# mLSTM cell and mixture of depths on one core: state products moved next to the product with P, second gates spread over two steps, operands on ScalarE, a reordered tail

## The chip, the core and the metric

The kernel runs on one core of a Trainium2 chip. The time is that of the device for one launch, in microseconds; seven runs of the kernel before had a median of 219.94 us (218.05 to 221.98). Profiles come from one further execution, taken by the hardware profiler; its times are in us unless ns is written.

The core's engines, as the profile names them: PE (TensorE, matrix products; PEld is its load of the stationary operand), DVE (VectorE), ACT (ScalarE), POOL (GpSimd) and SP (SyncE, which here only issues DMAs). Each engine works through its own instructions in order, so an instruction that waits holds up all that stand behind it on the same engine.

## What is computed

Two stages. The first is an mLSTM cell over B = 4 batches, H = 8 heads, S = 768 tokens and head size D = 40:

```python
for t in range(S):
    m_new = np.maximum(f_gate[:, :, t] + m, i_gate[:, :, t])
    f_stab = np.exp(f_gate[:, :, t] + m - m_new)
    i_stab = np.exp(i_gate[:, :, t] - m_new)
    m = m_new
    C = f_stab[..., None, None] * C + i_stab[..., None, None] * np.einsum('bhd,bhe->bhde', vt, kt)
    n = f_stab[..., None] * n + i_stab[..., None] * kt
    h_tilde = np.einsum('bhde,bhe->bhd', C, qt)
    denom = np.maximum(np.abs(np.einsum('bhd,bhd->bh', n, qt)), 1.0)[..., None]
    y[:, :, t] = sigmoid(o_gate[:, :, t]) * h_tilde / denom
```

The second takes x = y with the heads side by side (B, S, 320). Each token gets a score, `x @ w_gate`; in each batch the 128 tokens of the highest score go through two dense layers (320 to 1024 to 320) and are replaced by `x + sigmoid(score) * (relu(x @ w1) @ w2)`; the others leave as they are.

## The kernel before

**Tiles.** A batch is cut into six chunks of 128 tokens. Chunk c of batch b is step n = 6b + c; there are 24 steps. Inside a chunk the recurrence is written as a product: `pS` = keys times queries (line 313), a weight matrix W per head with exponents from the gates, `P = pS * W` (line 319, VectorE), and `pH = P v` (line 367). What comes from earlier chunks is the state C: `pIC` holds C times the queries (line 339) and the chunk's own contribution to C (line 345). `num` on VectorE adds both (lines 349 and 374), lines 377 to 380 make the reciprocal of the denominator, `sor` on POOL multiplies it with the output gate (line 382), `x` (line 387) is the result, stored from SP, and `scr`/`sc` (line 390) its score.

**The gates.** They are scanned along tokens for 96 rows at once (three chunks of 32 heads), in two groups g = 0 and 1: running sums and maxima (lines 177 to 179), `ends`, `carry` and `carried` through PE, `level`, then `split` into three bfloat16 parts. `operands` (line 222) makes from these parts, by a product into `pO`, two operands per chunk and half of the batches: `a_o` (ScalarE) and `M_o` (VectorE, line 234). `weights` multiplies them (`pW`, line 291) and takes exponentials on ScalarE; `causal` on POOL zeroes what lies ahead in time (line 297). `columns` transposes the scales; `scaled_v` (POOL, line 304) gives `wv` for the state, and `decay` (POOL, line 327) scales C ahead of the addition on VectorE (lines 357 and 359).

**Selection and layers.** `spread` transposes the score column on PE (`pb`, line 396) and ScalarE copies it; `compare` counts in step n + 1 how many tokens lie above (line 403). At c = 0 of the next batch `columns_of`, `ranks` and `select` turn the counts into ranks and a selection matrix; at c = 1 `gather` makes the indices (`pidx`, line 431) and an indirect DMA on POOL fetches the 128 rows `xe`; at c = 2 they are transposed (`pX`, line 451); from c = 3 `first` (line 471, `ph`) and, in the batch after that, `second` (line 480, `py`) run a few products a step in `layer`; `leave` writes the rows back at c = 2. The last batch does all of this behind its last step. `warm` (line 173) are products whose result nobody reads, in steps without layer work.

**Order.** The schedule is written out by hand: each engine's instructions stand in the order in which the code issues them, and the tile pools put in the waits. In step n of the kernel before the order is: P(n), W(n+2) with causal and wv, state products and num of step n, decay, layer, pH(n), pb(n-1), transposes `pt` of step n+2 (line 271), pS(n+1), norm, compare, x, select or gate, operands. On-chip buffers matter: the PSUM pool `ps_m` has two buffers for pO, pb, ph, py, pX, pcol and pidx; `ps_t` two for pt and pW; `ps_h` one for pH and the warm products. Loads are issued four steps ahead, and the weights w1 and w2 in steps 3 to 7.

**Shapes on PE.** pH, pIC and the chunk's part of the state use all 128 rows and 64 columns at a time (128*64 in the profile), pS uses 64 rows (64*128), pW and pO 32 rows (32*128), and the rest the full array (128*128). All but pW, pO, warm, pcol and the steps' pidx are float32.

Of the kernel before, what the change touches and what calls it, by code (L numbers as in the profile page):

```python
# [27 lines left out]
def kernel(  # L28
# [127 lines left out]

    FM = [gate.tile([NR, 2, L], FP, name=f"FM{g}") for g in range(2)]
# [17 lines left out]
    def scans(g):  # L175

        nc.vector.tensor_tensor_scan(out=FM[g][:, 0], data0=ones, data1=f_sb[g], initial=0.0, op0=OP.mult, op1=OP.add)
        nc.vector.tensor_tensor(out=a[g], in0=i_sb[g], in1=FM[g][:, 0], op=OP.subtract)
        nc.vector.tensor_tensor_scan(out=FM[g][:, 1], data0=ones, data1=a[g], initial=-BIG, op0=OP.mult, op1=OP.max)

# [41 lines left out]
    def operands(u, c):  # L222
# [4 lines left out]
        for j in (1, 0):  # L227
            for part in range(3):
# [5 lines left out]
        nc.vector.scalar_tensor_tensor(out=M_o[u, c], in0=pO[0].unsqueeze(1).to_broadcast([128, 4, L]),  # L234
                                       scalar=of[:, 1:2], in1=which.unsqueeze(2).to_broadcast([128, 4, L]),
                                       op0=OP.add, op1=OP.mult)

    def columns(g):
# [3 lines left out]
        for j, row in enumerate((wk[g], r[g], r[g][:, L - 1:L].to_broadcast([NR, L]))):  # L242
            nc.tensor.transpose(pc[:, j, :], row, ident[0:NR, 0:NR])
        both = const.tile([128, 3, NR], FP, name=f"cols{g}")
# [86 lines left out]
    def exchange(b, c, qk, T, wv):  # L331
# [9 lines left out]
        if c < NT - 1:  # L341

            for p in range(NP):
                for j, e in enumerate(HALVES):
                    nc.tensor.matmul(pC[e, p, :], qk[:, 0, 2 * p + j, :], wv[:, 2 * p + j, :], start=True, stop=True)  # L345
        num = None
# [81 lines left out]
    def gather(b, sel, token):  # L428
        pidx = ps_m.tile([K_, 1], FP, name="pidx", tag="m")
        for t in range(NT):  # L430
            nc.tensor.matmul(pidx, sel[:, t, :], token[:, t:t + 1], start=(t == 0), stop=(t == NT - 1))
        idx = mod.tile([K_, 1], U32, name="idx")
# [79 lines left out]
    def layer(b, c):  # L512

        if b > 0 and c == 1:
            picked[b - 1] = gather(b - 1, sel[b - 1], token)
        elif b > 0 and c == 2:
# [14 lines left out]
        elif c == 4:  # L531
            layers[b - 1].first(3, 7)
        else:
            layers[b - 1].first(7, NFC)
            layers[b - 1].second(0, 5)

    def step(n):
        b, c = steps[n]
        qk, v1, so = loaded[n]
        load(n + AHEAD)  # L540
        P = weighted(pS[n], W[n])
        if n + 2 < N:
            W[n + 2] = weights(*steps[n + 2])
            causal(W[n + 2])
            stated(n + 2)
        num = exchange(b, c, qk, T[n], wv[n])
        if n + 1 < N:
            decay(*steps[n + 1])
        layer(b, c)
        pH = within(P, v1)  # L550
        pb, pc = steps[n - 1]
        spread(pc, *state[pb][1][:2])
# [181 lines left out]
```

## Time and profile before

| | |
|---|---|
| median of seven runs | 219.94 us (218.05 to 221.98) |
| the profiled execution | 217.27 us |
| its span, first to last instruction | 214.80 us |
| PE busy | 188.9 us (88%) |
| DVE busy | 139.4 us (65%) |
| POOL busy | 99.3 us (46%) |
| ACT busy | 94.1 us (44%) |
| mean granted clock of PE | 0.956 |
| start of pH in steps 1, 6, 12, 18, 23 | 29.7, 64.9, 110.7, 150.8, 185.9 us |

A line of the timeline gives the start, the length, the engine, the source line, the operation, output <- inputs, the shape and how many instructions are taken together; in brackets stands how long the engine was idle before and which instruction it waited for. Matmuls overlap, so the difference of two starts says more than a length. A row `PEclk` holds the clock that PE was granted, in 40 equal slices of the span (5.37 us each), 9 for full speed.

### The profile page before, as it was taken

What the parts mean: (1) busy time and instruction counts of PE and PEld (TensorE: products, weight loads), DVE (VectorE), ACT (ScalarE), POOL (GpSimd) and SP (SyncE); (2) the same over time, 40 slices, a digit from 0 to 9 for tenths busy, and PEclk for the clock granted to TensorE, in tenths of its full rate; (3) what the DMA queues carried; (4) which work ended last, traced back from release to release, by engine and by line L of the source; (5) the groups of instructions that cost most, each with busy time, mean ns of one, the idle gap of its engine ahead of it and who ended that gap; (6) DMA issues with size and microseconds to landing.
All of it is one profiled execution on the core that took longest, in us unless ns stands there. A gap on an engine that the chain in (4) does not pass through costs nothing.

```text
span 214.8 us, 6507 instructions
## 1 busy us (share of the span) xinstructions
PE 188.9 (88%) x2611; PEld 152.2 (71%) x2611; DVE 139.4 (65%) x414; ACT 94.1 (44%) x212; POOL 99.3 (46%) x152
## 2 busy tenths in 40 slices
PE   7978698797898949999999999999999999848991
PEld 2556476675677737889877879988878899638970
DVE  6655737669877962856778668676786875662101
ACT  5762816443664441654645543566525541100110
POOL 6172547445556571344476555554585441021101
PEclk9987859999999995999999999999999999999998
DMA  4899994796999899759599897589992010000100
GB/s 84 119 169 145 149 170 90 95 132 171 134 197 171 212 169 220 125 56 146 104 160 137 129 124 158 94 137 140 142 136 69 34 61 3 31 32 34 31 0 31
DMA packets 105854, 24.37 MB, mean 113 GB/s; under 512 B 100640, under 2 KB 105248, under 8 KB 105824
## 3 DMA queue, kind: packets, MB, share of 16 engines
q1 hardware_dynamic: 105296, 22.60, 69.2%
q0 software_dynamic: 384, 1.31, 2.0%
q8 instruction: 20, 0.33, 0.8%
q14 instruction: 10, 0.08, 0.1%
q10 hardware_dynamic: 144, 0.05, 0.1%
HBM read 19.37 MB, written 4.59 MB: 112 GB/s over the span
## 4 chain that ended last, share of the span: by engine, by line
PE 63%; DVE 12%; issue 10%; DMA 5%; POOL 5%; ACT 2%; POOLq 1%; DVEq 0%
PE pH L367 12%; PE pS L313 9%; PE ph L471 8%; PE pt L271 7%; PE pIC L339 6%; PE py L480 6%; PE pw L173 5%; DMA xe<-out_dram,idx 4%; POOL sor L382 4%; PE pIC L345 4%; PE pW L291 3%; PE pb L396 2%; DVE x L387 1%; DVE scr L390 1%; DVE sel L425 1%
## 5 line engine op out<-in xcount | busy, mean ns | idle before, releaser
L382 POOL TENSOR_TENSOR sor<-so,rec 128x320 f32<-128x320 f32 x24 | 24.2, 1007 | 49.3 <-DVE rec L380 45.0
L297 POOL TENSOR_SCALAR_AFFINE_SELECT W<-W 128x512 f32<-128x512 f32 x48 | 31.5, 681 | 29.8 <-ACT W L292 29.8
L367 PEld LDWEIGHTS pH<-v,P 128*64 128x64 f32 x768 | 27.0, 148 | 12.2 <-PE pw L173 6.1
L397 ACT COPY sb<-pb 128x128 f32<-128x128 f32 x24 | 6.4, 266 | 64.1 <-PE pb L396 56.6
L367 PE MATMUL pH<-v,P 128*64 128x64 f32 x768 | 30.4, 237 | 3.4 <-PE pw L173 1.6
L319 DVE TENSOR_TENSOR P<-pS,W 128x512 f32<-128x512 f32 x48 | 30.7, 680 | 0.0
L292 ACT ACTIVATE W<-pW 128x512 f32<-128x512 f32 x48 | 26.0, 594 | 6.4 <-PE pW L291 5.1
L272 ACT COPY T<-pt 128x512 f32<-128x512 f32 x48 | 25.9, 588 | 5.8 <-PE pt L271 5.8
L313 PE MATMUL pS<-T 64*128 64x128 f32 x384 | 27.9, 285 | 0.0
L271 PE MATMUL pt<-ident,qk 128*128 128x128 f32 x192 | 26.1, 280 | 0.7 <-ACT W L292 0.7
L313 PEld LDWEIGHTS pS<-T 64*128 64x128 f32 x384 | 23.3, 187 | 4.0 <-issue 3.9
L374 DVE TENSOR_TENSOR num<-num,pH 128x328 f32<-128x328 f32 x20 | 9.9, 496 | 23.0 <-PE pH L367 23.0
L471 PE MATMUL ph<-xeT,w 128*128 128x128 f32 x192 | 24.1, 280 | 0.3 <-DVE idx L433 0.3
L271 PEld LDWEIGHTS pt<-ident,qk 128*128 128x128 f32 x192 | 22.6, 145 | 1.5 <-ACT W L292 1.0
L471 PEld LDWEIGHTS ph<-xeT,w 128*128 128x128 f32 x192 | 22.2, 192 | 1.0 <-issue 0.4
L480 PE MATMUL py<-w,hT 128*128 128x320 f32 x64 | 19.1, 438 | 0.0
L387 DVE TENSOR_TENSOR x<-num,sor 128x320 f32<-128x320 f32 x20 | 9.8, 492 | 13.2 <-POOL sor L382 13.2
L339 PE MATMUL pIC<-C,T 128*64 128x82 f32 x320 | 16.4, 246 | 0.0
L339 PEld LDWEIGHTS pIC<-C,T 128*64 128x64 f32 x320 | 13.0, 140 | 4.2 <-issue 2.5
L403 DVE SCALAR_TENSOR_TENSOR ge<-sb,sc,earlier 128x128 bf16<-128x128 f32 (+5 forms) x24 | 15.4, 643 | 0.8 <-ACT sb L397 0.8
L327 POOL TENSOR_TENSOR C<-C,cols 128x328 f32<-128x328 f32 x16 | 11.8, 736 | 6.8 <-DVE C L359 5.7
L173 PE MATMUL pw<-earlier 128*128 128x512 bf16 x38 | 13.5, 470 | 1.6 <-POOL earlier L98 1.6
(124 smaller groups left out, 265.2 us busy)
## 6 DMA issues: line engine op xcount, KB each, us to landing
qk<-in_k_dram SPq DMA_DIRECT2D x24, 160.0 KB, 3.4
qk<-in_q_dram SPq DMA_DIRECT2D x24, 160.0 KB, 4.0
v<-in_v_dram SPq DMA_DIRECT2D x24, 160.0 KB, 4.4
so<-in_o_gate_dram SPq DMA_DIRECT2D x24, 160.0 KB, 4.4
out_dram<-x SPq DMA_DIRECT2D x24, 160.0 KB, 2.2
w<-in_moe_w_dram SPq DMA_DIRECT2D x2, 640.0 KB, 4.7
w<-in_moe_w_dram SPq DMA_DIRECT2D x2, 512.0 KB, 3.9
w<-in_moe_w_dram SPq DMA_DIRECT2D x1, 256.0 KB
```

What stands on the lines that cost most here:

```text
L173: nc.tensor.matmul(pw, earlier[:, 0:128], earlier[:, 0:4 * L], start=True, stop=True)
L271: nc.tensor.transpose(pt[:, p, :], qk[:, j, 2 * p:2 * p + 2, :].rearrange("s a d -> s (a d)"), ident)
L272: nc.scalar.copy(out=T[:, j], in_=pt)
L292: nc.scalar.activation(out=W[:, h0:h0 + 4, :], in_=pW, func=AF.Exp)
L297: nc.gpsimd.affine_select(out=W[:, h0:h0 + 4, :], in_=W[:, h0:h0 + 4, :], compare_op=OP.is_ge, fill=0.0, base=0, pattern=[[0, 4], [1, L]], ...
L313: nc.tensor.matmul(pS[j][:, p, :], T[e, 0, p, :], T[e, 1, p, :], start=True, stop=True)
L319: nc.vector.tensor_tensor(out=P[:, :, j, :], in0=pS[j], op=OP.mult, in1=W.rearrange("p (n a) t -> p n a t", a=2)[:, :, j, :])
L339: nc.tensor.matmul(pI[t, 2 * p * D1:2 * (p + 1) * D1], T[:, 1, p, t], C[:, p].rearrange("e a d -> e (a d)"), start=True, stop=True)
L367: nc.tensor.matmul(pH[t, 2 * p + j, :], P[:, p, j, t], v1[:, 2 * p + j, :], start=True, stop=True)
L382: nc.gpsimd.tensor_tensor(out=sor, in0=so, in1=rec.unsqueeze(2).to_broadcast([128, H, D]), op=OP.mult)
L471: nc.tensor.matmul(self.ph[:, f % 4, :], w1[:, j, f * 128:(f + 1) * 128], self.xeT[:, j, :], start=(j == 0), stop=(j == NDC - 1))
L480: nc.tensor.matmul(self.py, self.hT[:, f, :], w2[:, f, :], start=(f == 0), stop=(f == NFC - 1))
```

## The change

The order of a step is turned: step n begins with pH(n), directly behind it come the state products of step n+1 (`exchange`, now without its VectorE part, which is `exchanged`), decay(n+1) and pS(n+1). Then W(n+2) and operands, norm, compare, x, then columns_of or gather, layer, pt(n+2), pb(n) (one step earlier than it was), and at the end P(n+1), num(n+1) and the addition to C. In steps 1 to 3 W(n+2) is computed late, behind pb. Nine of the twelve M_o (chunks 3 to 5 of the first two batches, all of the last two) are made by four ScalarE activations, one per head (`beside=False`). The second group's gates, which stood ahead of step 1, are cut into pieces that run inside steps 0 and 1. The placement matrices for the second half of the batches are built behind step 2 instead of step 1. In the tail, `leave` of batch 2 and a second selection matrix in half precision stand ahead of the copies, and the indices come from the latter.

The diff, with one line around each changed place:

```diff
                                 in_=ident.rearrange("p (g x) -> p g x", x=32)[:, :, 12 * j:12 * j + 12])
+    of_which = const.tile([128, 4], FP, name="of_which")
+    nc.vector.tensor_scalar(out=of_which, in0=which, scalar1=of[:, 1:2], scalar2=None, op0=OP.mult)
     FM = [gate.tile([NR, 2, L], FP, name=f"FM{g}") for g in range(2)]
...
             nc.tensor.matmul(pw, earlier[:, 0:128], earlier[:, 0:4 * L], start=True, stop=True)
-    def scans(g):
+    def sums(g):
         nc.vector.tensor_tensor_scan(out=FM[g][:, 0], data0=ones, data1=f_sb[g], initial=0.0, op0=OP.mult, op1=OP.add)
         nc.vector.tensor_tensor(out=a[g], in0=i_sb[g], in1=FM[g][:, 0], op=OP.subtract)
+    def maxima(g):
         nc.vector.tensor_tensor_scan(out=FM[g][:, 1], data0=ones, data1=a[g], initial=-BIG, op0=OP.mult, op1=OP.max)
...
         nc.scalar.activation(out=r[g], in_=FM[g][:, 1], func=AF.Exp, bias=m_in[g], scale=-1.0)
-    def operands(u, c):
+    def operands(u, c, beside=True):
         g, own = c // 3, slice(c % 3 * BH, c % 3 * BH + BH)
...
         nc.scalar.activation(out=a_o[u, c], in_=pO[1], func=AF.Identity, bias=of[:, 0:1], scale=1.0)
-        nc.vector.scalar_tensor_tensor(out=M_o[u, c], in0=pO[0].unsqueeze(1).to_broadcast([128, 4, L]),
-                                       scalar=of[:, 1:2], in1=which.unsqueeze(2).to_broadcast([128, 4, L]),
-                                       op0=OP.add, op1=OP.mult)
+        if beside:
+            nc.vector.scalar_tensor_tensor(out=M_o[u, c], in0=pO[0].unsqueeze(1).to_broadcast([128, 4, L]),
+                                           scalar=of[:, 1:2], in1=which.unsqueeze(2).to_broadcast([128, 4, L]),
+                                           op0=OP.add, op1=OP.mult)
+        else:
+            for h in range(4):
+                nc.scalar.activation(out=M_o[u, c][:, h], in_=pO[0], func=AF.Identity, scale=which[:, h:h + 1],
+                                     bias=of_which[:, h:h + 1])
     def columns(g):
...
             nc.tensor.transpose(pc[:, j, :], row, ident[0:NR, 0:NR])
+        return pc
+    def keep(g, pc):
         both = const.tile([128, 3, NR], FP, name=f"cols{g}")
...
                     nc.tensor.matmul(pC[e, p, :], qk[:, 0, 2 * p + j, :], wv[:, 2 * p + j, :], start=True, stop=True)
+        return pI, pC
+    def exchanged(b, c, pI, pC):
         num = None
...
                                 in1=rank[:, t0:t1].unsqueeze(2).to_broadcast([128, t1 - t0, K_]), op=OP.is_equal)
-    def gather(b, sel, token):
+    def number(sel, token):
         pidx = ps_m.tile([K_, 1], FP, name="pidx", tag="m")
...
             nc.tensor.matmul(pidx, sel[:, t, :], token[:, t:t + 1], start=(t == 0), stop=(t == NT - 1))
+        return pidx
+    def gather(b, pidx):
         idx = mod.tile([K_, 1], U32, name="idx")
...
     def layer(b, c):
-        if b > 0 and c == 1:
-            picked[b - 1] = gather(b - 1, sel[b - 1], token)
-        elif b > 0 and c == 2:
+        if b > 0 and c == 2:
             layers[b - 1] = Layers(b - 1, *picked[b - 1])
...
         elif c == 4:
-            layers[b - 1].first(3, 7)
+            layers[b - 1].first(3, NFC)
         else:
-            layers[b - 1].first(7, NFC)
             layers[b - 1].second(0, 5)
-    def step(n):
+    def weighed(n):
+        causal(W[n])
+        stated(n)
+    def step(n, **more):
         b, c = steps[n]
-        qk, v1, so = loaded[n]
+        _, v1, so = loaded[n]
         load(n + AHEAD)
-        P = weighted(pS[n], W[n])
-        if n + 2 < N:
+        pH = within(P[n], v1)
+        for f in more.get("carry", ()):
+            f()
+        if n + 1 < N:
+            give = exchange(*steps[n + 1], loaded[n + 1][0], T[n + 1], wv[n + 1])
+            decay(*steps[n + 1])
+            pS[n + 1] = products(T[n + 1])
+        late = 0 < n < NT - 2
+        if 1 < n < NT - 2:
+            operands(0, n + 2, beside=False)
+        if n + 2 < N and not late:
             W[n + 2] = weights(*steps[n + 2])
-            causal(W[n + 2])
-            stated(n + 2)
-        num = exchange(b, c, qk, T[n], wv[n])
-        if n + 1 < N:
-            decay(*steps[n + 1])
+        if 4 <= n < 4 + NT:
+            operands(1, n - 4, beside=False)
+        num, sor = norm(nums.get(n), pH, so)
+        for f in more.get("sor", ()):
+            f()
+        if n > 0:
+            pb, pc = steps[n - 1]
+            compare(pc, *state[pb][1])
+        if c == 0:
+            state[b] = open_batch()
+        result(b, c, num, sor, state[b][0])
+        for f in more.get("result", ()):
+            f()
+        if b > 0 and c == 0:
+            pcol = columns_of(state[b - 1][1][2])
+        elif b > 0 and c == 1:
+            picked[b - 1] = gather(b - 1, number(sel[b - 1], token))
         layer(b, c)
-        pH = within(P, v1)
-        pb, pc = steps[n - 1]
-        spread(pc, *state[pb][1][:2])
         if n + 2 < N:
...
             gated(n + 2)
+            if not late:
+                weighed(n + 2)
+        spread(c, *state[b][1][:2])
+        if late:
+            W[n + 2] = weights(*steps[n + 2])
         if n + 1 < N:
-            pS[n + 1] = products(T[n + 1])
-        num, sor = norm(num, pH, so)
-        compare(pc, *state[pb][1])
-        if b > 0 and c == 0:
-            pcol = columns_of(state[b - 1][1][2])
-        if c == 0:
-            state[b] = open_batch()
-        result(b, c, num, sor, state[b][0])
+            P[n + 1] = weighted(pS[n + 1], W[n + 1])
+            nums[n + 1] = exchanged(*steps[n + 1], *give)
+        for f in more.get("end", ()):
+            f()
+        if late:
+            weighed(n + 2)
         if b > 0 and c == 0:
...
                 layers[b - 2].leave()
-        if n + 3 < NT:
-            operands(0, n + 3)
-        if 3 <= n < 3 + NT:
-            operands(1, n - 3)
     state[0] = open_batch()
...
     load(4)
-    pS = {}
+    P, pS, nums, kept = {}, {}, {}, {}
     warm(8)
-    scans(0)
+    sums(0)
+    maxima(0)
     ends(0)
...
     turn(loaded[0][0], 1, T[0])
-    columns(0)
+    operands(0, 1)
     W[0] = weights(0, 0)
-    warm(1)
+    keep(0, columns(0))
+    weighed(0)
     pS[0] = products(T[0])
-    operands(0, 1)
-    causal(W[0])
-    stated(0)
     gated(0)
-    scans(1)
-    P = weighted(pS[0], W[0])
+    P[0] = weighted(pS[0], W[0])
     W[1] = weights(0, 1)
-    split(1, 1, 0, nc.gpsimd.tensor_copy, nc.gpsimd)
-    split(1, 1, 1, nc.gpsimd.tensor_copy, nc.gpsimd)
-    causal(W[1])
-    ends(1)
+    weighed(1)
     turned(1)
-    warm(1)
-    exchange(0, 0, loaded[0][0], T[0], wv[0])
-    carry(1)
-    pH = within(P, loaded[0][1])
+    give = exchange(0, 0, loaded[0][0], T[0], wv[0])
+    exchanged(0, 0, *give)
     operands(0, 2)
-    pm = carried(1)
-    pS[1] = products(T[1])
-    num, sor = norm(None, pH, loaded[0][2])
-    stated(1)
-    decay(0, 1)
-    level(1, pm)
-    W[2] = weights(0, 2)
-    split(1, 0, 0, nc.scalar.copy, nc.vector)
-    result(0, 0, num, sor, state[0][0])
-    split(1, 0, 1, nc.scalar.copy, nc.vector)
-    causal(W[2])
-    stated(2)
-    scales(1)
     gated(1)
-    turned(2)
-    operands(0, 3)
-    columns(1)
-    gated(2)
     nc.gpsimd.affine_select(out=earlier[:, S - L:], in_=earlier[:, S - L:], compare_op=OP.is_gt, fill=0.0, base=0,
                             pattern=[[-1, L]], channel_multiplier=1)
-    for n in range(1, N):
+    def parts_of_a():
+        for half in range(2):
+            split(1, 1, half, nc.gpsimd.tensor_copy, nc.gpsimd)
+    def level_and_split():
+        level(1, kept["pm"])
+        scales(1)
+        split(1, 0, 0, nc.vector.tensor_copy, nc.vector)
+    def rest_of_M():
+        split(1, 0, 1, nc.vector.tensor_copy, nc.vector)
+        operands(0, 3, beside=False)
+        kept["pc"] = columns(1)
+    step(0, sor=[lambda: sums(1), parts_of_a], result=[lambda: maxima(1), lambda: ends(1)], end=[lambda: carry(1)])
+    step(1, carry=[lambda: kept.update(pm=carried(1))], sor=[level_and_split], result=[rest_of_M],
+         end=[lambda: keep(1, kept["pc"])])
+    for n in range(2, N):
         step(n)
-        if n == 1:
+        if n == 2:
             for j in range(2):
...
             nc.vector.tensor_copy(out=token, in_=token_i)
-            token_f = const.tile([128, NT], FP, name="token_f")
-            nc.vector.tensor_copy(out=token_f, in_=token_i)
             later = const.tile([128, NT], FP, name="later")
-            nc.vector.tensor_scalar(out=later, in0=token_f, scalar1=-1.0, scalar2=float(S - 1), op0=OP.mult, op1=OP.add)
+            nc.vector.tensor_scalar(out=later, in0=token_i, scalar1=-1.0, scalar2=float(S - 1), op0=OP.mult, op1=OP.add)
             ones_b = const.tile([128, 1], BF, name="ones_b")
...
     own = layers[b - 1]
-    spread(u, sc, sb)
     compare(u, sc, sb, ge, cnt)
...
             nc.tensor.matmul(pX[0:w, j, :], x_t[b, t][:, d0:d0 + w], sel[:, t], start=(t == 0), stop=(t == NT - 1))
+    own.leave()
+    sel_h = mod.tile([128, NT, K_], HF, name="sel", bufs=1)
+    select(sel_h, rank, 0, NT)
     nc.scalar.copy(out=last.xeT[:, 0:NDC - 1], in_=pX[:, 0:NDC - 1])
     nc.scalar.copy(out=last.xeT[0:w, NDC - 1], in_=pX[0:w, NDC - 1])
-    own.leave()
-    last.idx, last.xe = gather(b, sel, token_f)
+    last.idx, last.xe = gather(b, number(sel_h, token))
     last.first(0, NFC)
```

## The prediction

> Steps are numbered n = 0 to 23 (six per batch); pH(n) is step n's product with P, "state" the two blocks L339/L345 (pIC and pC). Times are us of the span.
>
> **What bounds the kernel now.** I first read the busy times and the clock row of the page: PE is busy 88%, but its clock was halved three times (slices 3 to 6, 16 and 17; the tails of the row are full speed).
>
> ```profile
> PE 188.9 (88%) x2611; PEld 152.2 (71%) x2611; DVE 139.4 (65%) x414; ACT 94.1 (44%) x212; POOL 99.3 (46%) x152
> PEclk9987859999999995999999999999999999999998
> ```
>
> Then the chain in order of time, for the starts of pH: pH(0) 16.2, pH(1) 29.7, then 37.8, 45.2, 52.5, 58.8, 64.9, 72.4, 82.7, 91.8, 98.9, 104.7 and pH(12) 110.7; pH(18) 150.8; pH(23) 185.9; end 214.8. So there are four regimes, each with its own limit. Steps with expert layers are full on PE; the timeline of one:
>
> ```profile
> 98.78 1.15 PE L367 MATMUL pH<-v,P 128*64 128x64 f32 x32
> 99.86 0.32 PE L396 MATMUL pb<-ident,sc 128*128 128x128 f32 x1
> 100.02 1.04 PE L271 MATMUL pt<-ident,qk 128*128 128x128 f32 x8
> 100.99 1.16 PE L313 MATMUL pS<-T 64*128 64x128 f32 x16
> 102.08 0.39 PE L291 MATMUL pW<-M_o,a_o 32*128 32x512 bf16 x2
> 102.40 0.79 PE L339 MATMUL pIC<-C,T 128*64 128x82 f32 x16
> 103.12 1.60 PE L471 MATMUL ph<-xeT,w 128*128 128x128 f32 x12
> 104.65 1.15 PE L367 MATMUL pH<-v,P 128*64 128x64 f32 x32
> ```
>
> Differences of starts are what each block costs: pH 1.08, pb 0.16, pt 0.97, pS 1.09, pW 0.32, pIC 0.72, ph 1.53 (2.21 for x18). No gap is left. The shape changes six times in a step, and the first instructions behind a change are slower: inside the pt block six transposes take 0.65 (100.02 to 100.67), so eight should take 0.87, not 0.97; inside ph two take 0.22, so 18 should take 1.98, not 2.21.
>
> In batch 0 PE waits. There a loop on VectorE closes through PE: scr(n), M_o 0.74, pW, pIC, state, warm, pH(n+1), num:
>
> ```profile
> 42.04 0.75 DVE L234 SCALAR_TENSOR_TENSOR M_o<-pO,of,which 128x512 bf16<-128x512 f32 x1
> 42.84 0.39 PE L291 MATMUL pW<-M_o,a_o 32*128 32x512 bf16 x2 [1.25 <-DVE M_o L234]
> ```
>
> At n=8 PE waits for a gather, and the clock falls behind it (pH(8) takes 2.0 instead of 1.1):
>
> ```profile
> 74.83 1.23 POOL L435 DMA_INDIRECT xe<-out_dram,idx  x1 [0.36 <-DVE den L378]
> 80.49 0.88 PE L451 MATMUL pX<-ident,xe 128*128 128x128 f32 x3 [3.15 <-DMA xe<-out_dram,idx]
> ```
>
> The tail is a chain on PE: pX 4.3, pidx 1.5, ph 5.5, py 4.5, then ye and its write.
>
> ```profile
> 198.26 1.50 PE L431 MATMUL pidx<-token_f,sel 128*128 128x1 f32 x12
> 200.10 5.60 PE L471 MATMUL ph<-xeT,w 128*128 128x128 f32 x48 [0.34 <-DVE idx L433]
> ```
>
> **The change, stage by stage.**
>
> *Shapes.* In the new order pH(n), pIC(n+1) and state(n+1) share one shape, and ph, pt, pb another: pH/pIC/pC, pS, pW, full block. Four changes instead of six. The two that go are pW to pIC and pH to pb. By the excesses above a change costs 0.10 (pt block) to 0.23 (ph block, both ends); I take 0.15 each, 0.3 a step. Two new pairs (state to pS, pW to ph) are in no row; bounds for the sum are 0 and 0.45 (two at the larger excess).
> The Trainium skill (TensorEngine Tiling (Array Packing), Key Properties) says that a change of tiling mode drains the array, which agrees and gives no price; by it alone the sum would stay open.
>
> *Steady steps.* A full step is then pH 1.07 + pIC 0.56 + state 0.45 + pS 1.09 + pW 0.30 + ph 2.19 + pt and pb 0.98 = 6.64 (was 6.99). It holds only if VectorE's loop is shorter: after P(n) ends, L349 and C take 1.06 (0.41 + 0.65), num 0.53, den/den/rec 0.6, sor on POOL 1.0 to 1.4 with its hand-overs 0.15, x and scr 1.05, P(n+1) 1.2: 5.5 to 5.9. Hidden under PE in full steps. By c: c=0: pcol 0.79 and py 1.75 in place of ph: 7.0. There pb now waits for rank, since pcol holds the other of two buffers; rank stands behind P, num and C on VectorE, about 6.65 after P(n), and pH(n+1) is queued behind pb. PE arrives there at 6.9, so py covers it; uncovered it costs up to 1. c=1: 6.67. c=2: 6.26. c=3: ye and scre moved behind P, so the write of ye (1.04 on POOL) and decay 0.74 stand before sor: 7.2, not 6.64. c=4 (no state): 6.19. c=5 (ph x12, no pIC): 5.42 on PE, 5.5 on VectorE. Batch sum 38.8 against 40.1 (110.7 to 150.8). Steps 18 to 22: 7.0+6.67+6.26+7.2+6.4 = 33.5 against 35.1.
>
> *Operands.* Nine of twelve M_o go from VectorE (0.74) to ScalarE: four activations of 128x128, by the a_o row (0.36) 1.44, bounds 1.1 and 1.5. VectorE's loop in batch 0 loses 0.74. But in n=4 to 9 a_o and M_o stand behind two exponentials (1.1), and what comes next on PE (pcol, pidx, pX, ph) needs a_o's buffer: pO done at 3.9 behind the start of pH, a_o at 4.6, hence 0.7 of PE wait in n=6 to 9 (bounds 0 and 0.9). T follows M_o on ScalarE and is now wanted 1.2 after pt: about 0.1 late.
>
> *Start.* Without the second gates PE reaches pH(0) at 14.5, pH(1) at 21 (was 29.7): P(0) no longer stands behind the scans (it began at 13.38; now at 11.6, behind causal). In step 0 the scans (1.1) and in step 1 level and splits (1.9) stand on VectorE's chain; pO(3) waits for M's last split until 26.5, M_o until 28.3, T copies to 29.65, pW(3), pH(2) at 30.1 (was 37.8).
>
> *Steps 2 to 4.* Here the lead goes back. In the late steps pW(n+2) comes behind pt and shares its two buffers: it waits for T's copies (0.7 behind pt). Its exponentials stand on ScalarE behind so (0.95) and sb (0.27); then causal (0.65 behind) and wv (0.74) on POOL. From pt: 0.7+0.95+0.27+1.1+0.65+0.74 = 4.4. State(n+2), in front of pS on PE, wants wv at 2.6: 1.8 of PE wait, where the trace of before has none. A step is then 8.3 to 8.8. Places (33.59 to 35.88 before: 2.3 on POOL) moved one step later, in front of decay and sor(3): that step 9.7. The three casts behind n=3 (0.31+0.62+0.6) wait for iota behind causal: step 4 7.9. pH(3) 38.9, pH(4) 48.6, pH(5) 56.5 (was 58.8).
>
> *Queues and small things.* SP's order stays: load(n+4), x, then w1 or w2; x and the loads behind it move with the steps, qk of n+1 is read a step earlier, and a load has two steps before pt wants it (landing 3.4 to 6.4), so I cost it at nothing, though w2's second half now leaves beside the gather. of_which (one VectorE row of 0.15) falls into the wait for f_sb (0.63); the removed cast token_f (0.16) and two warm products (0.39 each) are inside the sums.
>
> *Steps 5 to 11.* 5: 5.85 (VectorE). 6: 7.3 (pO 0.42 and rank). 7: 6.75. 8: 6.7 and 0.95 of waits. 9: 6.64+0.42+0.7 = 7.76. 10: 6.19. 11: 5.5. The gather now leaves at the end of step 7 (idx behind scr) instead of in its middle; pX comes 5.4 behind it, and the trace's one loaded gather took 5.66, so 0.3 of wait instead of 3.15, bounds 0 and 3. pH(9) 84.1 (was 91.8), pH(12) 103.5 (was 110.7).
>
> *Tail.* With the half-precision sel and token pidx costs what it does in the steps (0.30 for x6 at 71.32) instead of 1.50. The new select (0.96) and ye stand beside pX (4.3). ph then waits for xeT (198.99): 1.1 earlier.
>
> **The sum.**
>
> | | before | after |
> |---|---|---|
> | pH(2) | 37.8 | 30.1 |
> | pH(5) | 58.8 | 56.5 |
> | pH(9) | 91.8 | 84.1 |
> | pH(12) | 110.7 | 103.5 |
> | pH(18) | 150.8 | 142.3 |
> | pH(23) | 185.9 | 175.9 |
> | end | 214.8 | 203.7 |
>
> That is at full clock. Before, the clock was halved in 14.9 to 18.3, 25.1 to 31.9 and 79.7 to 86.5, each time behind about 3.4 us in which PE was busy some 55% or less (the stretch 77.4 to 80.5 shows no matmul at all). After, steps 1 to 4 have such stretches (24.6 to 26.5, 31.7 to 33.5, 40.5 to 42.2). pH(1), 2.0 for 1.1, prices one halving at 1.5 to 3. I take 3 in sum, bounds 0 and 8.
> The Trainium skill (TensorE: Matmul & The Clock Gate, Part 1) says that an idle window of about 3.4 us halves the clock and a busy one of that length gives it back; it speaks against this change, which adds idle time to steps 1 to 4. By its wording a partly busy window might cost nothing or all, so by it the span would lie anywhere from 203.7 to 211.7.
>
> So span 206.7, and with the 2.47 around it (217.27 - 214.80) 209.2, 3.7% under the profiled 217.27. That execution lies under all seven runs (218.05 to 221.98); scaled to their median 219.94 it is 211.7. I say **211.5**.
>
> **Rivals.**
> 1. *Forecast* (0.48): 207 to 215.
> 2. *Clock holds and wv comes in time* (0.16): 203.7 + 2.5, scaled, is 208.7; without the 0.7 waits in n=6 to 9 and half the 1.8 waits 204. For it: more PE work between gaps in the start.
> 3. *The lead of the start is given back whole* (0.14): halved clock in each of steps 1 to 4 (8) and the gather late by 3: 203.7+8+2.7 = 214.4, with the ends 216.9, scaled 219.5. No change.
> 4. *Slower: the clock stays low* (0.22). Place: from step 1 to pH(9), where ph begins. Before, the busy stretch 25.1 to 28.5 with small gaps did not give the clock back; the new waits for wv, T and a_o leave gaps in every such step. If it stays halved past pH(4), each of steps 4 to 8 costs some 3 more: 203.7+3+15 = 221.7, 224.2 with the ends, scaled 227. It decides from the third halved step on. Against it: steps 5 to 8 are nearly full on PE by the sums above, and the before kernel recovered in two stretches.
>
> A change of under 1% is what a measurement of this kernel hardly tells from none. Cases 1 and 2 are faster and 4 is slower; of case 3's 0.14 I put 0.02 to faster, 0.11 to same and 0.01 to slower: faster 0.66, same 0.11, slower 0.23. The range takes in case 2, the forecast and case 3: 204 to 221.
>
> **What would show it.** pIC directly behind pH with no slow first rows; steps of 6.6 at c=3, 4 in batch 1, and 7.2 at c=3 of batch 2; PE waiting in front of L358 for wv in steps 2 and 3 (right: 1 to 2); pb at c=0 waiting for rank by little; pX at n=8 waiting under 1; pidx at 0.3. I am wrong if the clock row shows more than three halved slices, if ScalarE ends waits in the steady steps, or if the gather still ends a wait of 3.

## Result and the profile after

The changed kernel takes **209.75 us** (median of 20 runs, 208.13 to 211.28), the kernel before 219.14 (48 runs, 215.80 to 222.57): a ratio of 0.9617, 95% interval 0.9590 to 0.9644. The ratio, here and in the experiments, compares only runs within 1.5% of the fastest of their kernel; 209.75 over 219.14 would be 0.957. The forecast was 211.5, with a range of 204 to 221. The profiled execution of the changed kernel has a span of 208.2 us at a mean granted clock of 0.969 and took 210.24 us.

First the page: the rows of busy time and of the granted clock (40 slices, tenths of full speed).

```profile
PE 183.6 (88%) x2606; PEld 150.3 (72%) x2606; DVE 143.6 (69%) x408; ACT 102.8 (49%) x246; POOL 100.1 (48%) x152
...
PEclk9999966999999999969999999999999999999997
```

PE is as busy a share of a shorter span. Two places are slower in the clock row, slices 6 and 7 and slice 18; before there were three.

Then the chain of PE, one step with experts (n = 10, the step that was shown of before; start, duration, engine, line):

```profile
94.13 1.15 PE L383 MATMUL pH<-v,P 128*64 128x64 f32 x32
95.11 0.74 PE L352 MATMUL pIC<-C,T 128*64 128x82 f32 x16
95.78 1.16 PE L326 MATMUL pS<-T 64*128 64x128 f32 x16
96.88 0.39 PE L304 MATMUL pW<-M_o,a_o 32*128 32x512 bf16 x2
97.19 2.27 PE L491 MATMUL ph<-xeT,w 128*128 128x128 f32 x18
99.31 1.04 PE L284 MATMUL pt<-ident,qk 128*128 128x128 f32 x8
100.18 0.27 PE L412 MATMUL pb<-ident,sc 128*128 128x128 f32 x1
100.38 1.15 PE L383 MATMUL pH<-v,P 128*64 128x64 f32 x32
```

By differences of starts: pH 0.98 (was 1.08), pt 0.87 (0.97), ph for 18 products 2.12 (2.21). The blocks whose neighbour now has their own shape are each 0.1 shorter.

The waits of PE that answer to those of before, from its timeline (in brackets the idle time ahead, and what ended it):

```profile
42.86 0.67 PE L358 MATMUL pIC<-wv,qk 128*64 128x41 f32 x16 [1.50 <-POOL wv L317]
...
82.14 0.55 PE L471 MATMUL pX<-ident,xe 128*128 128x128 f32 x3 [1.36 <-ACT a_o L238]
...
89.31 3.90 PE L491 MATMUL ph<-xeT,w 128*128 128x128 f32 x18 [1.16 <-ACT a_o L238]
...
192.81 0.30 PE L448 MATMUL pidx<-token,sel 128*128 128x1 f16 x6
193.46 5.59 PE L491 MATMUL ph<-xeT,w 128*128 128x128 f32 x48 [0.34 <-ACT xeT L734]
```

The 3.15 us for the gather are gone from pX; in their place stands 1.36 for a_o. The same kind of wait stands ahead of pcol (1.14), pidx (1.36) and ph (1.16), and behind the last the clock is halved: 3.90 for what takes 2.27 a step later.

Where the 6.6 us of span went, by the starts of pH:

| stretch | before | after | difference | forecast (full clock) |
|---|---|---|---|---|
| to pH(5) | 58.8 | 55.9 | -2.9 | 56.5 |
| pH(5) to pH(9) | 33.0 | 28.3 | -4.7 | 27.6 |
| pH(9) to pH(12) | 18.9 | 21.8 | +2.9 | 19.4 |
| pH(12) to pH(18) | 40.1 | 39.9 | -0.1 | 38.8 |
| pH(18) to pH(23) | 35.1 | 34.4 | -0.7 | 33.6 |
| pH(23) to the end | 28.9 | 27.8 | -1.1 | 27.8 |

The forecast's column sums to 203.7; with its 3 us for the clock it was 206.7, against 208.2.

### The profile page after: what moved, and what is told of

It is laid out like the page before. It is cut to its first block, busy times and chain, and to the rows that moved or that the text cites. A ratio compares the mean times of both kernels' runs of the same rounds, so it can differ in the third digit from the quotient of the medians.

```text
span 208.2 us, 6517 instructions
## 1 busy us (share of the span) xinstructions
PE 183.6 (88%) x2606; PEld 150.3 (72%) x2606; DVE 143.6 (69%) x408; ACT 102.8 (49%) x246; POOL 100.1 (48%) x152
## 4 chain that ended last, share of the span: by engine, by line
PE 34%; DVE 18%; issue 10%; POOL 7%; ACT 3%; DMA 3%; POOLq 1%; ACTq 0%
PE pH L383 7%; PE ph L491 6%; PE pS L326 5%; PE pt L284 4%; POOL sor L398 4%; PE py L500 3%; DVE P L332 3%; PE pIC L352 3%; ACT W L305 3%; DVE scr L406 2%; DVE x L403 2%; DVE num L390 2%; DVE ge L419 2%; DVE den L394 2%; DMA out_dram<-ye,idx 1%
## 5 line engine op out<-in xcount | busy, mean ns | idle before, releaser
L310 POOL TENSOR_SCALAR_AFFINE_SELECT W<-W 128x512 f32<-128x512 f32 x48 | 32.7, 704 | 30.9 <-ACT W L305 30.5
L383 PEld LDWEIGHTS pH<-v,P 128*64 128x64 f32 x768 | 25.7, 141 | 7.6 <-DVE P L332 2.7
L383 PE MATMUL pH<-v,P 128*64 128x64 f32 x768 | 29.2, 230 | 1.9 <-DVE P L332 1.9
L491 PE MATMUL ph<-xeT,w 128*128 128x128 f32 x192 | 25.4, 292 | 1.5 <-ACT a_o L238 1.2
L491 PEld LDWEIGHTS ph<-xeT,w 128*128 128x128 f32 x192 | 23.7, 203 | 3.2 <-issue 1.4
L403 DVE TENSOR_TENSOR x<-num,sor 128x320 f32<-128x320 f32 x20 | 11.1, 553 | 12.7 <-POOL sor L398 12.7
L419 DVE SCALAR_TENSOR_TENSOR ge<-sb,sc,earlier 128x128 bf16<-128x128 f32 (+5 forms) x24 | 17.9, 746 | 1.0 <-ACT sb L413 1.0
L317 POOL TENSOR_TENSOR wv<-v,cols 128x328 f32<-128x328 f32 x20 | 15.0, 751 | 0.0
L358 PE MATMUL pIC<-wv,qk 128*64 128x41 f32 x320 | 12.9, 230 | 1.9 <-POOL wv L317 1.9
L406 DVE CUSTOM_DVE_ANT_0 scr<-x,wg 128x320 f32<-128x320 f32 x24 | 14.0, 582 | 0.8
```

The lines of the kernel that those rows point to most:

```text
L310: nc.gpsimd.affine_select(out=W[:, h0:h0 + 4, :], in_=W[:, h0:h0 + 4, :], compare_op=OP.is_ge, fill=0.0, base=0, pattern=[[0, 4], [1, L]], ...
L383: nc.tensor.matmul(pH[t, 2 * p + j, :], P[:, p, j, t], v1[:, 2 * p + j, :], start=True, stop=True)
L419: nc.vector.scalar_tensor_tensor(out=ge[:, GE[u]:GE[u + 1]], in0=sb.rearrange("p t l -> p (t l)")[:, 0:n], scalar=sc[:, u:u + 1], in1=earl ...
L491: nc.tensor.matmul(self.ph[:, f % 4, :], w1[:, j, f * 128:(f + 1) * 128], self.xeT[:, j, :], start=(j == 0), stop=(j == NDC - 1))
```

## Experiments

Each kernel was timed beside the kernel before on the same chip; "ratio" is its time over that one, with the 95% interval, to be held against 0.9617. Steps are differences of pH starts. Where a half-speed stretch falls is different in each execution, so a step is compared with the same step at full clock, and spans are compared at equal mean clock.

### 1. a_o ahead of the exponentials

```
-        if n + 2 < N and not late:
-            W[n + 2] = weights(*steps[n + 2])
         if 4 <= n < 4 + NT:
             operands(1, n - 4, beside=False)
+        if n + 2 < N and not late:
+            W[n + 2] = weights(*steps[n + 2])
```

> The edit: in steps 4 to 9 pO, a_o and M_o are issued ahead of pW and its two exponentials, instead of behind them. Theory A (the 1.1 to 1.4 us that PE waits ahead of pcol, pidx, pX and ph at n = 6 to 9 are the two exponentials that stand ahead of a_o on ScalarE): these four waits, 5.0 us in sum in the changed kernel, fall to 0.4 or less each, nothing else grows by more than it had in slack, and a halved clock behind the wait at n = 9 (ph 3.90 instead of 2.27) goes with it. Time 209.75 - 3.5 to - 6 = 204 to 206. Rival B (VectorE's loop of 5.5 to 5.9 us, or the exponentials and causal, now 1.9 later, end the wait instead): the waits move to pH (behind P) or to L358 (behind wv), and the time stays within 1.5 us of 209.75.

206.62 us, ratio 0.9503 (0.9413 to 0.9593). PE's timeline of this kernel around n = 8 and 9:

```profile
80.78 0.55 PE L471 MATMUL pX<-ident,xe 128*128 128x128 f32 x3 [0.28 <-ACT a_o L238]
...
82.66 1.15 PE L284 MATMUL pt<-ident,qk 128*128 128x128 f32 x8 [0.69 <-ACT W L305]
...
87.83 2.27 PE L491 MATMUL ph<-xeT,w 128*128 128x128 f32 x18
```

The waits for a_o fall to 0.28 or less, as theory A has it. But pt now waits for the buffers that the exponentials free, since M_o's 1.5 us stand ahead of them on ScalarE (4.5 us in sum over steps 4 to 8). Steps 6 to 9 sum to 28.56; the changed kernel's 7.74, 6.94, 7.81 and, at full clock, 8.26 (experiments 2, 5, 6 and 9) sum to 30.75. So of 5.0 us of waits 2.2 were won; step 5 even grew, by 0.77 (6.60), for the same wait of pt (1.40). At a clock of 0.991 to 0.992 its spans are 204.7 to 204.8, the changed kernel's 206.2 to 206.5. This execution had one half-speed window of 3.41 us, the changed kernel's three. The order on ScalarE was the cause of the waits; that half of the gain goes into the next wait is the rival's part.

### 2. scre and ye ahead of P at c = 2

```
+        if b > 0 and c == 2:
+            layers[b - 1].gate()
+            if b > 1:
+                layers[b - 2].leave()
         if n + 1 < N:
             P[n + 1] = weighted(pS[n + 1], W[n + 1])
...
-        elif b > 0 and c == 2:
-            layers[b - 1].gate()
-            if b > 1:
-                layers[b - 2].leave()
```

> The edit: at c = 2 scre and ye stand ahead of P(n+1) on VectorE, as in the kernel before. Theory A (the 7.35 and 6.98 us of steps c = 3 and c = 4 in the third batch come from ye's late write: it holds POOL, decay and sor run late, and VectorE's small operations beside them are stretched, 2.4 us in that step): step c = 2 grows by 0.5 (P starts 1.04 later, with 0.5 of slack), step c = 3 falls to about 6.65 and step c = 4 to about 6.3, because P no longer comes 0.53 late nor C 0.38: -0.9 in each of the last two batches, time 207.5 to 208.5. Rival B (c = 3 is long because VectorE has more to do, wherever ye stands): the sum of the three steps stays at 20.4 and the time within 0.5 of 209.75.

209.10 us, ratio 0.9579 (0.9505 to 0.9653): by time no difference to be told. By steps of the third batch: c = 2 6.38 (was 6.05), c = 3 7.43 (7.35), c = 4 6.25 (6.98); in sum 20.06 instead of 20.38. First the changed kernel's step c = 3, VectorE and GpSimd in its timeline:

```profile
127.84 1.04 POOL L506 DMA_INDIRECT out_dram<-ye,idx  x1 [1.64 <-DVE ye L504]
...
128.20 0.74 DVE L394 SCALAR_TENSOR_TENSOR den<-num,den 128x8 f32<-128x8 f32 x1
128.91 0.74 POOL L340 TENSOR_TENSOR C<-C,cols 128x328 f32<-128x328 f32 x1
...
129.10 1.65 DVE L419 SCALAR_TENSOR_TENSOR ge<-sb,sc,earlier 128x384 bf16<-128x384 f32 x1
129.60 0.72 POOL L398 TENSOR_TENSOR sor<-so,rec 128x320 f32<-128x320 f32 x1
...
130.33 1.75 POOL L310 TENSOR_SCALAR_AFFINE_SELECT W<-W 128x512 f32<-128x512 f32 x2
...
130.68 0.90 DVE L403 TENSOR_TENSOR x<-num,sor 128x320 f32<-128x320 f32 x1
131.62 0.80 DVE L406 CUSTOM_DVE_ANT_0 scr<-x,wg 128x320 f32<-128x320 f32 x1
```

and the same rows in the timeline of this experiment:

```profile
129.53 0.17 DVE L394 SCALAR_TENSOR_TENSOR den<-num,den 128x8 f32<-128x8 f32 x1
...
129.85 0.57 DVE L419 SCALAR_TENSOR_TENSOR ge<-sb,sc,earlier 128x384 bf16<-128x384 f32 x1
...
131.04 0.49 DVE L403 TENSOR_TENSOR x<-num,sor 128x320 f32<-128x320 f32 x1 [0.60 <-POOL sor L398]
131.56 0.49 DVE L406 CUSTOM_DVE_ANT_0 scr<-x,wg 128x320 f32<-128x320 f32 x1
```

The late write of ye and decay do put GpSimd's work onto VectorE's, and den, ge, x and scr take 4.09 instead of 1.72. That part of theory A is shown, and c = 4 is repaired. But c = 3 is not: P now comes late at the end of c = 2: pH starts on its first half and waits for the second, then pIC waits 0.38 for C, and pIC starts 1.66 behind pH instead of 0.98. scre and ye stand on VectorE's loop in either place; rival B holds for most of the sum.

### 3. pb behind the next pH

```
         pH = within(P[n], v1)
+        if n > 0:
+            pb, pc = steps[n - 1]
+            spread(pc, *state[pb][1][:2])
...
-        spread(c, *state[b][1][:2])
```

> The edit: the transpose pb of a step goes back behind the next step's pH, between pH and pIC, where the kernel before had it. Six changes of array shape in a full step again instead of four; nothing else moves. Theory A (a change of shape costs PE about 0.15 us): a full step on PE is 0.3 longer (6.46 becomes 6.75 at c = 1, 6.05 becomes 6.35 at c = 2 of the third batch), some 4 us in all where PE is the bound, less what pb no longer waits for scr (0.70, 1.72 and 0.27 in steps 4, 5, 6): 211 to 214. Rival B (the change of shape costs nothing that counts, and the gain of the third and fourth batch came from elsewhere): steps c = 1 and c = 2 keep their 6.46 and 6.05, and the time is 207 to 210.

207.99 us, ratio 0.9529 (0.9440 to 0.9618). PE in this kernel's timeline at n = 16:

```profile
131.26 1.04 PE L284 MATMUL pt<-ident,qk 128*128 128x128 f32 x8
...
132.23 1.15 PE L383 MATMUL pH<-v,P 128*64 128x64 f32 x32
...
133.31 0.32 PE L412 MATMUL pb<-ident,sc 128*128 128x128 f32 x1
133.56 0.79 PE L352 MATMUL pIC<-C,T 128*64 128x82 f32 x16
```

pt takes 0.97, pH 1.08 and pb 0.25, against 0.87, 0.98 and 0.20 in the changed kernel. Steps c = 1 and c = 2 become 6.75 and 6.34 (6.45 and 6.05): **0.30 for two changes of shape, the 0.15 each of the forecast**. Yet the kernel is not slower: c = 3 is 6.99 instead of 7.35, c = 4 6.55 instead of 6.98, steps 2 to 4 lose 0.15 to 0.18 each at full clock, and its spans are 206.2 to 206.5 at a clock of 0.991 to 0.992, like the changed kernel's, and 204.8 at 0.997. So rival B is wrong on the price, theory A on the sum. Where the time at c = 3 went stands in this kernel's timeline of that step (n = 15):

```profile
129.64 0.48 DVE L403 TENSOR_TENSOR x<-num,sor 128x320 f32<-128x320 f32 x1
...
129.98 1.47 POOL L310 TENSOR_SCALAR_AFFINE_SELECT W<-W 128x512 f32<-128x512 f32 x2 [0.69 <-ACT W L305]
...
131.15 1.27 DVE L332 TENSOR_TENSOR P<-pS,W 128x512 f32<-128x512 f32 x2
```

GpSimd's selects (causal) wait 0.69 for the exponentials here, so that x takes 0.48 instead of 0.90. VectorE also begins num 1.20 behind pH(15) instead of 1.48, and P begins 5.9 behind it instead of 6.6. That pb's wait for scr cost anything is not shown: P stands behind scr on VectorE and pH needs P. Ahead of pH(5) the changed kernel waits 1.72 for scr and 0.26 for P; here, with pb out of the way, PE waits 2.13 in front of pH, until the first half of P is done.

### 4. wv ahead of causal

```
     def weighed(n):
-        causal(W[n])
         stated(n)
+        causal(W[n])
```

> The edit: on POOL, wv(n+2) stands ahead of the two causal selects of step n instead of behind them; it reads only v and the gate columns. Theory A (PE waits in front of L358 at n = 3 and n = 8, 1.50 and 0.42 us, for wv's place in POOL's queue behind causal, which itself waits for the late exponentials): both waits go, steps 3 and 8 are shorter by that, and no other wait takes their place: 207.5 to 208.5. Rival B (the time goes into the next wait, C or P on VectorE, or causal is now late for P): the two waits go and the time stays within 0.7 of 209.75.

208.29 us, ratio 0.9561 (0.9481 to 0.9640). Steps 2 and 3 fall to 6.64 and 7.60 (8.46 and 8.37): the waits were POOL's order. But at c = 3 of the later batches the step grows from 7.35 to 8.76. There causal has moved to where VectorE works (timeline of this kernel):

```profile
126.58 2.81 DVE L419 SCALAR_TENSOR_TENSOR ge<-sb,sc,earlier 128x384 bf16<-128x384 f32 x1
...
127.08 0.72 POOL L398 TENSOR_TENSOR sor<-so,rec 128x320 f32<-128x320 f32 x1
127.76 1.21 POOL L310 TENSOR_SCALAR_AFFINE_SELECT W<-W 128x512 f32<-128x512 f32 x2
```

ge, 0.57 in experiment 2, ends 0.42 behind the last select. c = 5 grows too, from 5.70 to 6.22; step 8 falls from 7.81 to 7.17. The time is inside theory A's range, but other waits did take the place of those that went: the edit is right in the late steps and in step 8, and wrong at c = 3 and c = 5 of the later batches.

### 5. The tail as before

```
-    own.leave()
-    sel_h = mod.tile([128, NT, K_], HF, name="sel", bufs=1)
-    select(sel_h, rank, 0, NT)
     nc.scalar.copy(out=last.xeT[:, 0:NDC - 1], in_=pX[:, 0:NDC - 1])
     nc.scalar.copy(out=last.xeT[0:w, NDC - 1], in_=pX[0:w, NDC - 1])
-    last.idx, last.xe = gather(b, number(sel_h, token))
+    own.leave()
+    last.idx, last.xe = gather(b, number(sel, token_f))
```

> The edit: of the tail alone, pidx goes back to the single-precision sel and token, and ye back behind xeT. Theory A (single-precision pidx costs 1.50 on PE instead of 0.30, and ph is queued behind it): ph starts 0.85 to 1.2 later behind pX, the run is longer by that at the same clock: 210.6 to 211. Rival B (ph waits for xeT anyway, so pidx lies beside that wait): ph starts at most 0.3 later, the time stays within 0.4 of 209.75.

211.29 us, ratio 0.9730 (0.9701 to 0.9759). PE's timeline at the end of this kernel:

```profile
192.57 1.50 PE L448 MATMUL pidx<-token_f,sel 128*128 128x1 f32 x12
194.41 5.60 PE L491 MATMUL ph<-xeT,w 128*128 128x128 f32 x48 [0.34 <-DVE idx L453]
```

From the start of pX (188.27 here, 188.51 in the changed kernel) to ph it is 6.14 instead of 4.95: 1.19, theory A. (The time is 0.3 above the range that theory A gave.)

### 6. M_o on VectorE in steps 2 to 9

```
-            operands(1, n - 4, beside=False)
+            later_M.append(operands(1, n - 4))    # a_o at once, M_o as a closure
...
         result(b, c, num, sor, state[b][0])
+        for M in later_M:
+            M()
```

> The edit: for steps 2 to 9 M_o is made by one VectorE instruction behind scr, ahead of P, instead of by four on ScalarE; the a_o stay where they are, behind the exponentials. Theory A (VectorE's loop is what steps 4 to 9 end on, so 0.74 more on it is 0.74 more a step): these six steps grow by 0.5 to 0.74 each, 3 to 4.4 us, 213 to 214. Rival B (in these steps PE's waits for a_o and for the late wv set the pace and VectorE has slack): steps 6 to 9 grow by 0.3 or less each, 4 and 5 by up to 0.74: 210 to 211.5.

208.41 us, ratio 0.9587 (0.9529 to 0.9645). Step 4 grows from 7.92 to 8.59; steps 7, 8 and 9 are 6.94, 7.95 and 8.26 (6.94, 7.81, 8.26), and step 6 is 7.55 (7.74); step 5 holds a half-speed stretch here. Rival B, and the time is below even its range: while PE waits for a_o, VectorE has the 0.74 to spare. At a clock of 0.983 the spans are 207.2 and 208.1, the changed kernel's 208.0 to 208.1. Moving these eight M_o to ScalarE gained nothing that can be measured.

### 7 and 8. The repairs together, and pb one step late

Experiment 7 joins 1, 3 and, for the late steps alone, 4. Experiment 8 leaves pb in the full block, but on the scores of the step before:

```
         pH = within(P[n], v1)
+        if b > 0 and c == 0:
+            spread(NT - 1, *state[b - 1][1][:2])
...
-        spread(c, *state[b][1][:2])
+        if c > 0:
+            spread(c - 1, *state[b][1][:2])
...
+        if c > 1:
+            compare(c - 2, *state[b][1])
+        elif b > 0 and c == 0:
+            for pc in (NT - 2, NT - 1):
+                compare(pc, *state[b - 1][1])
```

> The edit: a_o ahead of the exponentials in steps 4 to 9, pb behind the next pH, and wv ahead of causal in the three late steps alone. Theory A (the three waits are separate: a_o in steps 6 to 9, scr ahead of pH in every step, wv in steps 2 and 3): against a span of 206.4 of the changed kernel at clock 0.992, -3 for a_o, -1.5 for pb and -1.5 to -2.5 for wv: a span of 199.5 to 201.5 at full clock, 202 to 204.5 in time. Rival B (they free the same slack, and VectorE's loop takes its place in batch 0): 205 or more.

> The edit: as the three repairs, but pb stays in the full-array block and takes the scores of the step before, which are long there; its comparison follows a step later, and only a batch's last pb stands behind the next pH, with two comparisons in that step. Four shape changes a step, and nothing in front of pH waits for scr. Theory A (0.15 for a shape change, and pb's wait for scr was what ate it): steps c = 1 and 2 of the later batches 6.45 and 6.05, c = 3 6.65, c = 4 about 6.3, against 6.75, 6.34, 6.99 and 6.55 with pb behind pH; 1.2 a batch: 2.5 to 3.5 us under the kernel with the three repairs, 199 to 201.5. Rival B (VectorE, with the second comparison at c = 0 and the stretch beside GpSimd, ends these steps): c = 0 grows from 7.25 to 8, and the time is no lower than with the three repairs.

Experiment 7: 205.24 us, ratio 0.9466 (0.9421 to 0.9511), span 203.4 at clock 0.987: by time in the rival's range, though step 1 holds a half-speed stretch of 1.5 us (9.97 against 8.47 in experiment 8). What took the place of the waits is not mainly VectorE's loop, as the rival had it (0.69 for P in one step), but pt behind the exponentials, 5.0 us in steps 4 to 8. Experiment 8: **202.36 us, ratio 0.9302 (0.9247 to 0.9357)**, span 199.7 at full clock. Its steps in the third batch are 7.35, 6.45, 6.05, 7.26, 6.98, 5.57 against 7.25, 6.75, 6.34, 6.99, 6.55, 5.81: the shapes are won back at c = 1 and 2, but c = 3 and 4 did not fall as theory A said. There P was late by VectorE's own work (experiment 2), not by pb. The sum of the batch is 39.67 against 39.69 in experiment 7 and 39.94 in the changed kernel, so the 2.9 us under experiment 7 are not the gain that theory A forecast: steps 3 to 11 are 1.5 shorter together, and pH(3) is 2.3 earlier, most of it the half-speed stretch that this execution does not have. At a clock of 0.990 to 0.992 the spans are 203.3 to 203.4 and 201.4. With a_o out of the way the gather is seen again, in PE's timeline of experiment 8:

```profile
76.65 0.52 PE L471 MATMUL pX<-ident,xe 128*128 128x128 f32 x3 [0.79 <-DMA xe<-out_dram,idx]
```

In the four other kernels with a_o ahead (experiments 1, 7, 10 and 11) pX at n = 8 waits 0.28 for a_o and not for the gather.

### 9. The second gates up front

In front of step 0 stand sums, maxima, parts of a, ends, carry, level, splits of M, scales and columns; the callbacks of steps 0 and 1 go. This is not the order of the kernel before, where carried, level and the splits of M stood behind pH(0), which came at 16.0; here pH(0) comes at 21.3.

```
-    step(0, sor=[lambda: sums(1), parts_of_a], result=[lambda: maxima(1), lambda: ends(1)], end=[lambda: carry(1)])
-    step(1, carry=[lambda: kept.update(pm=carried(1))], sor=[level_and_split], result=[rest_of_M],
-         end=[lambda: keep(1, kept["pc"])])
-    for n in range(2, N):
+    for n in range(N):
```

> The edit: the second gates (sums, maxima, ends, carry, level, splits, scales, columns) are worked out ahead of step 0 again, as in the kernel before; all else as in the changed kernel. Theory A (the start is what the change gained, and steps 2 to 4 give back the part of it that my steps said): pH(1) comes at 28 to 30 instead of 21.4 and pH(2) at 35 to 37 instead of 31.2; the late steps then keep their waits for wv, so that pH(5) is at 59 to 62 instead of 55.9, and the time is 4 to 6 over the changed kernel: 213 to 216. Rival B (the late steps swallow the lead wholly, whatever the start): pH(5) within 1 us of 55.9, and the time within 1 of 209.75.

214.29 us, ratio 0.9803 (0.9741 to 0.9864). pH(1) at 28.3, pH(2) at 34.2, steps 2 to 4 8.37, 8.37 and 7.94 as in the changed kernel, pH(5) at 58.9: 2.9 behind the changed kernel, just under what theory A gave, while the time is within it. The lead of 6.9 at pH(1) is 2.9 at pH(5). What the span shows beyond that is the clock: half-speed stretches add 2.7 in steps 5 to 7 here, and the changed kernel's 1.6 in step 9 is missing, which gives 4.0 at pH(10) and at the end (212.2 against 208.2).

### 10 and 11. Two more on experiment 8

> The edit: the kernel with pb one step late, and M_o of steps 2 to 9 on VectorE behind scr, while a_o stays ahead of the exponentials on ScalarE. Theory A (what is left in steps 4 to 8 there, 4.9 us of pt waiting for the exponentials, comes from M_o's 1.5 us ahead of them on ScalarE; VectorE has that much slack): these waits go, steps 4 to 8 are 0.3 to 1.0 shorter each: a span of 196 to 197.5 at full clock instead of 199.7, a time of 198 to 200. Rival B (VectorE, at 0.74 more, becomes the bound: P waits): PE waits ahead of pH for P instead, span 199 to 201.

201.91 us, ratio 0.9269 (0.9199 to 0.9339), span 200.0 at full clock: the waits of pt in steps 4 to 8 go (4.3 in experiment 8, none here), and new ones for M_o ahead of pW (2.1 in two steps) and for P and C take their place. Rival B by the span; the wait for M_o it did not name.

> The edit: the kernel with pb one step late, and scre and ye ahead of P at c = 2. Theory A (P comes late at c = 3 and c = 4 because GpSimd's run of the write of ye, decay, sor and causal without a pause stretches VectorE's den, ge, x and scr, which work from SBUF to SBUF): with the write beside P and C instead, ge at c = 3 takes 0.57 to 0.7 instead of 1.65, den 0.17 instead of 0.74; c = 2 grows by at most 0.35, c = 3 falls from 7.26 to 6.65 to 7.0, c = 4 from 6.98 to 6.2 to 6.5: 0.5 to 1 us in each of the last two batches. Rival B (VectorE's sum of work is the limit over the three steps): c = 2 to c = 4 keep 20.3 in sum, and the span stays at 199.7.

**201.14 us, ratio 0.9216 (0.9164 to 0.9267)**, span 199.2 at full clock, the shortest of all. c = 2 to 4 are 6.38, 7.43 and 6.25, in sum 20.06 instead of 20.29: as in experiment 2, c = 4 is repaired and c = 3, for which theory A gave 6.65 to 7.0, is not. The gain over experiment 8 in the steps, 0.2 a batch, is too small for their times to tell.

## Why the prediction was right, point by point

**Shapes: right.** Four changes instead of six are worth 0.30 a full step (experiment 3), which was the step's 0.3.

**Steady steps: wrong.** The forecast had a batch of 38.8; it is 39.94, against 40.05 before. By c = 0 to 5 the steps miss the forecast by +0.40, -0.21, -0.21, +0.15, +0.79 and +0.20. The step that failed is the loop of VectorE, "5.5 to 5.9. Hidden under PE in full steps" (its terms add up to 5.6 to 6.0, and ge, which ran beside sor, is not among them). At c = 3 it is 6.6 from pH to P, by 2.4 us of stretched rows beside GpSimd; c = 3 is 7.35, near the 7.2 given, where the forecast had a later sor alone; but c = 4 then starts with a late P and C (6.98 instead of 6.19), and c = 0 likewise (7.40 instead of 7.0). The shapes' gain went there. With pb in front of pH, scr also stands on PE's queue in every step; taking that away (experiment 8) brought the batch only from 39.94 to 39.67.

**Operands: right in kind, too small.** The waits for a_o in n = 6 to 9 are 1.14, 1.36, 1.36 and 1.16, not 0.7 (bound 0.9): the exponentials begin 0.47 behind the start of pW (80.27, 80.74), and state comes up to 0.4 later by wv. The rows at n = 8:

```profile
80.27 0.39 PE L304 MATMUL pW<-M_o,a_o 32*128 32x512 bf16 x2
...
80.74 1.08 ACT L305 ACTIVATE W<-pW 128x512 f32<-128x512 f32 x2 [2.65 <-POOL sor L398]
...
81.71 0.37 ACT L238 ACTIVATE a_o<-pO,of 128x128 bf16<-128x128 f32 x1
```

Experiment 1 shows the cause. What was to be gained for it, VectorE's 0.74, was worth nothing (experiment 6).

**Start: right.** pH(0) 15.1, pH(1) 21.4, pH(2) 31.2 against 14.5, 21 and 30.1 at full clock; experiment 9 undoes it.

**Steps 2 to 4: right that the lead goes back, by somewhat too much.** 8.46, 8.37 and 7.92 against 8.8, 9.7 and 7.9; PE waits 1.50 for wv in step 3. The placements' 2.3 on POOL, put into step 3, did not show in its length (8.37, against 8.38 for step 2 at full clock).

**Gather: right.** 0.3 was given; none is seen, because a_o is later still. The gather left at 75.34; with the 5.66 us of the one before it would have landed at 81.0, 0.2 behind the end of pO, an estimate from these rows that fits the 0.3. In the five profiles with a_o ahead it was seen once, with 0.79 (experiment 8). The sign given for it, pX waiting under 1, failed for a_o's reason: 1.36.

**Tail: right**, 1.1 given, 1.19 measured.

**Clock: right in sum, partly by luck.** 3 was given; this execution lost 2.7, and the others lie between a span of 206.2 at 0.991 and one of 209.3 at 0.974. (In the kernel before the row has slice 16 halved; slice 17, which the prediction adds, is at full speed in it.) The stretch 28.1 to 34.9 costs 1.1 (step 1 9.77 instead of 8.74, step 2 8.46 instead of 8.38, where it hides the wait for wv), the stretch 89.5 to 92.9 1.62. Its place there was not foreseen.

So the 209.75 was met by errors of both signs: -1.6 in steps 2 to 4; +2.2 for a_o, +1.1 and +0.8 in the later batches, and some -0.7 in the rest of steps 5 to 11; at full clock the span came out 1.8 over the 203.7. The scaling from 209.2 to 211.5 also missed: it took the runs' median to lie above the profiled execution, as before the change, but 209.75 lies under the profiled 210.24. The likeliest case came true, but the gain that was put on the later batches' shapes (2.9) was only 0.9; what carried the change are the start (2.9), the stretch that held the gather's wait and the halved clock behind it (4.7), and the tail (1.1). The start and the tail are undone by experiments 9 and 5; no run puts the gather's wait back, so the 4.7 rests on the rows of before and after alone.

## What to carry to other kernels

When a reordering saves time on the full engine, work out the loop of the second engine with its neighbours' work beside it, step by step: the saving holds only in the steps where that loop is shorter. A block moved ahead in an in-order queue takes over its inputs' lateness in the profile: look whether the block behind it would have waited just as long (pH for P, experiment 3). Feeding it an older value gained 1.5 us over moving it (steps 3 to 11, experiments 7 and 8), and nothing where VectorE was the limit anyway. Where one engine makes operands for another, issue the one that frees a buffer first, and look at what the other then holds up: here that took half of the gain (experiment 1).

## What the runs showed of the hardware

VectorE rows with two inputs in SBUF were stretched while GpSimd worked without a pause: ge 0.57 to 1.65 and 2.81, den 0.17 to 0.74, x 0.49 to 0.90. P, which reads pS from PSUM and only W from SBUF, was not: each of its 48 halves in the changed kernel took 0.66 to 0.69. The Trainium skill (SBUF — State Buffer, Who interferes with whom) says that a VectorE instruction with two SBUF inputs contends with a GpSimd instruction that reads SBUF for a port pair that is locked by one of them at a time. These rows agree, and while the ge of 2.81 ran, GpSimd began three instructions in a row (sor and two selects).

All edges of half speed in the changed kernel's profile lie on one grid of 3.41 us (28.06, 34.89, 89.50, 92.92). The share in which PE was busy does not tell which window of the grid is followed by half speed: 59% (24.65 to 28.06) and 66% (86.09 to 89.50) were, 50% (51.95 to 55.37) was not. The changed kernel's runs fall into groups: spans of 206.2 to 206.5 at a clock of 0.991 to 0.992, 207.6 to 208.5 at 0.982 to 0.984, 209.3 at 0.974, and the profiled one, 208.2 at 0.969. The kernel before was never above 0.965 in the 26 runs beside the experiments. What a window must hold stays open.
